# Denominator product a tile sooner on GpSimd, and head sums and normalised queries ahead of the first gated slice on VectorE, in the middle tiles of the forward gated layers

## The chip, the cores and the metric

The kernel runs on one core of one Trainium2 chip. TensorE (PE; its weight loads are shown apart as PEld), VectorE (DVE), ScalarE (ACT) and GpSimd (POOL) each run a program of their own, in order; SyncE (SP) issues the DMAs. The metric is the device time of one execution in microseconds, and for several executions their median.

## The reference

A stack of four layers over x (2048 rows of 512, bfloat16): linear attention (A), gated unit (B), A, B, each on the normalised input and with a residual. Both A share their weights, and so do both B. The outputs are the result and the gradients of x and of the five weight matrices for a given gradient of the result.

```python
def _A_ref(x, wqkv, wo):                  # 32 heads of 16
    q, k, v = split(x @ wqkv)
    phi = lambda t: jnp.where(t > 0, t + 1, jnp.exp(t)) + 1e-6
    pq, pk = phi(q), phi(k)
    kv = jnp.einsum("bhsd,bhse->bhde", pk, v)
    z = jnp.einsum("bhsd->bhd", pk)
    num = jnp.einsum("bhqd,bhde->bhqe", pq, kv)
    den = jnp.einsum("bhqd,bhd->bhq", pq, z)[..., None] + 1e-6
    return heads_joined(num / den) @ wo

def _B_ref(x, w_gate, w_up, w_down):      # 512 -> 1376 -> 512
    g, u = x @ w_gate, x @ w_up
    return (_sigmoid(g) * u) @ w_down

x = x + _A_ref(_layernorm(x), A_wqkv, A_wo)
x = x + _B_ref(_layernorm(x), B_w_gate, B_w_up, B_w_down)
...
```

The part that matters here is `den`: for each row and head, the sum over 16 columns of pq times z, and the division by it.

## The kernel before

The rows are cut into 16 tiles of 128. The layers are numbered 0 (A), 1 (B), 2 (A), 3 (B). `kq_fwd` makes keys, queries and the sums of a whole A layer (`A.zb` holds z in every row, `A.pq_all` the queries). `ab_fwd` then runs over the 16 tiles of the following B layer and does the rest of the A layer a few tiles ahead of it. It runs once for layers 0 and 1 and once for 2 and 3. The backward passes and the weight gradients follow.

Inside `ab_fwd`, engines TensorE, VectorE, ScalarE and GpSimd are under a manual schedule: each runs its instructions in the order in which the code writes them. All DMAs of this part go through SP, in written order too. An instruction that waits holds up everything behind it on its engine.

The pieces, for tile `st` of the B layer:

- `A.prod(st + FLAG)`, with FLAG = 3: one product on GpSimd, pq times z for the tile three ahead, into one of two `prod` buffers (L840).
- `A.front1(st + FLAG)`: the sum over the 16 columns of each head, on VectorE (L846).
- `A.front2(st + FLAG)`: epsilon and reciprocal (L850, L851) and the queries times the reciprocal (`pqnstage`, L863), on VectorE; after every odd tile a DMA stores two tiles of them (L867).
- `A.front3(st + FLAG)`: four TensorE transposes of the normalised queries (L374) and a ScalarE copy (L383).
- `A.attn_y(st + YLAG)`, with YLAG = 2: four matmuls (L884), the residual add on VectorE (L892), and the normalisation sums of that tile: two instructions on VectorE (L449, L451) and three small ones on GpSimd (L452, L453, L455).
- `gu(T, hT, fs)`: one of three slices of the gated unit (512, 512 and 352 columns): gate and up matmuls into a `g` and a `u` bank of PSUM, two buffers each (L922); two sigmoids on ScalarE (L924, L926); up times sigmoid on VectorE, which frees the `u` bank (`hh_t`, L929); a product for the backward pass on GpSimd (`ssd_t`, L930).
- `finish(T)`: the down projection of a tile two before (L956) and its residual add on VectorE (L958). In layer 1 the normalisation sums for layer 2 follow (`nxt.stats`, again L449 to L455); in layer 3 there is no next layer and `nxt` is None.
- `ln.apply`, `ln.stage_T`: the normalised input of a coming tile, on ScalarE, and its transposes.
- `dma_T(T)`: the transpose of `hh_t` by DMA (L949), followed on SP by the stores of `ssd_t` and `hh_t` (L1051, L1052, L1054).

`by_dma` holds the middle tiles, 2 to 14, in both layers. For them the code begins with a memset of a pad of `hh_t` (L982); that tile has three buffers in layer 1 and two in layer 3, so the memset and the first slice may have to wait until the stores of an earlier tile are done. Tiles 0, 1 and 15 have an order of their own. `prod`, `front1` and `front2` do nothing for a tile number of 16 or more, so in middle tiles 13 and 14 they are empty.

Of the kernel before, what the change touches and what calls it, by code (L numbers as in the profile page):

```python
# [35 lines left out]
def fchunks_of_slice(fs):  # L36
    c0, w = FSL[fs]
    return list(range(c0 // P, (c0 + w + P - 1) // P))


def fc_rows(fc):
    return FLAST if fc == NFC - 1 else P


def rows(st):
    return slice(st * P, (st + 1) * P)
# [9 lines left out]
def ps_tile(k, which, shape, dt, name):  # L56
    return k.ps[which].tile(shape, dt, name=name, tag="ln_tp" if which == "ln" else f"{which}_ps")
# [766 lines left out]
FLAG = 3  # L824
# [78 lines left out]
def ab_fwd(k, A, ln, side, nxt=None, out_cb=None, last_cb=None):  # L903
    nc, tc = k.nc, k.tc
    la, l = A.l, A.l + 1
    sva, sv = k.sv[la], k.sv[l]
    with ExitStack() as ctx:
        work = ctx.enter_context(tc.tile_pool(name=f"bf_work{l}", bufs=2, reuse_waits="tile"))
        wide = ctx.enter_context(tc.tile_pool(name=f"bf_wide{l}", bufs=2, reuse_waits="tile"))
        if out_cb is not None:  # L910
            k.ostg = ctx.enter_context(tc.tile_pool(name="out0_stg", bufs=2, reuse_waits="tile"))

        by_dma = HH_DMA[l]

        def gu(T, hT, fs, later=False):
            c0, w = FSL[fs]
            ssd_t, hh_t = T["ssd"], T["hh"]
            g_ps = ps_tile(k, "g", [P, 512], F32, "g_ps")
            u_ps = ps_tile(k, "u", [P, 512], F32, "u_ps")
            for ps, w_sb in ((g_ps, k.wg), (u_ps, k.wu)):  # L920
                for kc in range(NDC):
                    nc.tensor.matmul(ps[:, 0:w], lhsT=hT[:, kc, :], rhs=w_sb[:, kc, c0:c0 + w],  # L922
                                     start=(kc == 0), stop=(kc == NDC - 1))
            nc.scalar.activation(ssd_t[:, 0, c0:c0 + w], g_ps[:, 0:w], ACT.Sigmoid)  # L924
            oms = work.tile([P, 512], BF16, name="oms")
            nc.scalar.activation(oms[:, 0:w], g_ps[:, 0:w], ACT.Sigmoid, scale=-1.0)  # L926

            def rest():
                nc.vector.tensor_tensor(hh_t[:, c0:c0 + w], u_ps[:, 0:w], ssd_t[:, 0, c0:c0 + w], ALU.mult)  # L929
                nc.gpsimd.tensor_tensor(ssd_t[:, 1, c0:c0 + w], hh_t[:, c0:c0 + w], oms[:, 0:w], ALU.mult)  # L930
            if later:
                return rest
            rest()

        def transposes(T, fs):
            hh_t, hhT = T["hh"], T["hhT"]
            fcs = fchunks_of_slice(fs)
            tps = ps_tile(k, "t", [P, 8, P], BF16, "t_tp")
            for i, fc in enumerate(fcs):
                r = fc_rows(fc)  # L940
                nc.tensor.transpose(tps[0:r, i, :], hh_t[:, fc * P:fc * P + r], k.ident[:])
            nfull = len([fc for fc in fcs if fc_rows(fc) == P])
            if nfull > 0:
                nc.scalar.copy(hhT[:, fcs[0]:fcs[0] + nfull, :], tps[:, 0:nfull, :])
            if nfull < len(fcs):
                nc.scalar.copy(hhT[0:FLAST, NFC - 1, :], tps[0:FLAST, nfull, :])

        def dma_T(T):
            nc.sync.dma_start(out=T["hhT"][:], in_=T["hh"][:], transpose=True)  # L949

        def finish(T, bank="y"):
            st = T["st"]
            y_ps = ps_tile(k, bank, [P, D], F32, "y_ps")
            for fc in range(NFC):
                r = fc_rows(fc)
                nc.tensor.matmul(y_ps[:], lhsT=T["hhT"][0:r, fc, :], rhs=k.wd[0:r, fc, :],  # L956
                                 start=(fc == 0), stop=(fc == NFC - 1))
            nc.vector.tensor_tensor(k.xs[st][:], y_ps[:], k.xs[st][:], ALU.add)  # L958
            if nxt is not None:
                nxt.stats(st)  # L960
            ready.append(st)

        ready = []

        def after(upto):
            while ready and ready[0] <= upto:
                st = ready.pop(0)
                if nxt is not None:
                    nxt.apply(st)
                if out_cb is not None:  # L970
                    out_cb(st)

        todo = []
        for st in range(NST):
            hT = ln.pop(st)
            T = dict(st=st,
                     ssd=wide.tile([P, 2, F], BF16, name="ssd_t"),
                     hh=wide.tile([P, FP], BF16, name="hh_t", bufs=3 if l == 1 else 2),
                     hhT=wide.tile([P, NFC, P], BF16, name="hhT"))
            late = st - 1 in by_dma or st in by_dma  # L980
            if st in by_dma:
                nc.gpsimd.memset(T["hh"][:, F:FP], 0.0)  # L982
                A.prod(st + FLAG)
                gu(T, hT, 0)
                A.attn_y(st + YLAG)
                A.front1(st + FLAG)
                A.front2(st + FLAG)
                if todo and todo[0]["st"] <= st - 1 - (st - 1 in by_dma):
                    finish(todo.pop(0), "t")
                after(st - 3)  # L990
                gu(T, hT, 1)
                ln.stage_T(st + 1, "scalar")
                gu(T, hT, 2)
            elif st == 0:
                rest0 = gu(T, hT, 0, True)
                A.front2(2)
                rest0()
                gu(T, hT, 1)
                ln.apply(1)
                A.front3(2, "t")  # L1000
                rest2 = gu(T, hT, 2, True)
                ln.stage_T(1)
                rest2()
                A.front1(FLAG)
                A.attn_y(2)
                transposes(T, 0)
                A.front2(FLAG)
            else:
                A.prod(st + FLAG)
                gu(T, hT, 0)  # L1010
                if st == 1:
                    ln.apply(YLAG)
                else:
                    A.attn_y(st + YLAG)
                if late:
                    finish(todo.pop(0), "t")
                after(st - 2 - late)
                gu(T, hT, 1)
                if st == 1:
                    A.front3(FLAG)  # L1020
                transposes(T, 0)
                if st == 1:
                    A.attn_y(FLAG)
                else:
                    ln.stage_T(st + 1)
                A.front1(st + FLAG)
                gu(T, hT, 2)
                if st == 1:
                    ln.stage_T(2)
                A.front2(st + FLAG)  # L1030
            if l == 1 and st == NST - 1:
                nc.scalar.activation(k.tab[:], k.neg[:], ACT.Exp)
            if st not in by_dma:
                transposes(T, 1)
            if st > 0:
                ln.apply(st + YLAG)
            if st == NST - 1:
                if last_cb is not None:
                    last_cb(0)
                if nxt is not None:  # L1040
                    nxt.early_T()
            if st not in by_dma and todo:
                after(st - 2)
                finish(todo.pop(0))
            if st > 0:
                A.front3(st + FLAG, "t" if st in by_dma else "ln")
            if st in by_dma:
                dma_T(T)
            else:
                transposes(T, 2)  # L1050
            nc.sync.dma_start(out=sv["ssd"][rows(st), :, :], in_=T["ssd"][:])  # L1051
            nc.sync.dma_start(out=sv["hdd"][0:NG, :, st, :].rearrange("g p w -> p g w"),  # L1052
                              in_=T["hh"][:, 0:NG * GW].rearrange("p (g w) -> p g w", g=NG))
            ins = nc.sync.dma_start(out=sv["hdl"][0, :, st, :], in_=T["hh"][:, NG * GW:F])  # L1054
            if st in side:
                with tc.issue_after(ins.ins):
                    side[st]()
            todo.append(T)
        if out_cb is not None:
            out_cb(NST - 2)  # L1060
        if last_cb is not None:
            last_cb(1)
        finish(todo.pop(0))
        if out_cb is not None:
            out_cb(NST - 1)
# [838 lines left out]
```

## Time and profile before

| | us |
|---|---|
| median of 3 runs | 1137.57 |
| the three runs | 1137.09, 1137.57, 1140.26 |
| profiled execution, its own time | 1138.25 |
| its span, first to last instruction | 1136.5 |

| instruction in the profile | count | median ns |
|---|---|---|
| L840 product, GpSimd | 30 | 1153 |
| L846 head sums, VectorE | 32 | 654 |
| L850 epsilon, VectorE | 32 | 181 |
| L851 reciprocal, VectorE | 32 | 353 |
| L863 normalised queries, VectorE | 32 | 692 |

The forward gated layers take the stretches from about 70 to 206 us and from about 262 to 400 us of the span. Times below are microseconds from the start of the span. A row of the timeline gives start, duration, engine, line, operation, the tile written and those read, and in brackets the engine's idle time before it and what ended it. "x2" is two neighbours shown as one row. VectorE's instructions overlap a little, so the distance from start to start is shorter than the duration.

### The profile page before, as it was taken

The page shows a single profiled execution, that of the slowest core. Times are in us where ns is not written, and L with a number is a line of the kernel's source. Part 1 is how long each engine was busy: PE and PEld are TensorE (multiplying, and loading weights), DVE is VectorE, ACT ScalarE, POOL GpSimd, SP SyncE. Part 2 cuts the span into 40 slices and gives each one's busy share as a digit, 9 for nine tenths or more (in the row PEclk, how much of TensorE's full clock was granted, in tenths as well). Part 3 has the DMA queues.
Part 4 walks back from the last instruction along what each step waited for, and adds up shares of the span by engine and source line. Part 5 has one row for each costly group of instructions (what it writes and reads, how often), then busy time and mean ns, then how long its engine had stood idle before and what let it go on. Part 6 is the DMA issues. An engine that isn't in the chain of part 4 may idle for free. (4 is left out here: it accounts for less than half of the span.)

```text
span 1136.5 us, 20007 instructions
## 1 busy us (share of the span) xinstructions
PE 1112.9 (98%) x7468; PEld 650.7 (57%) x7468; DVE 696.3 (61%) x1344; ACT 483.8 (43%) x909; POOL 292.9 (26%) x518
## 2 busy tenths in 40 slices
PE   8989999998999999999999999999999999999998
PEld 4444554444545555554446468855547745448887
DVE  6787876777667466664975850166674976951111
ACT  6666666555755633433625431224324515410000
POOL 5647776435666400000110220000000111210000
PEclk9999999999999999999999999999999999999999
DMA  8967999855899989997899997799998899979996
GB/s 270 310 194 213 288 263 277 250 141 174 228 267 286 269 260 254 303 260 201 224 263 310 220 254 234 210 277 287 248 286 256 209 276 291 239 200 298 266 194 187
DMA packets 413682, 282.36 MB, mean 248 GB/s; under 512 B 198608, under 2 KB 399504, under 8 KB 409744
## 3 DMA queue, kind: packets, MB, share of 16 engines
q1 hardware_dynamic: 413584, 281.08, 89.8%
q8 instruction: 58, 0.95, 0.3%
q14 instruction: 40, 0.33, 0.1%
HBM read 125.44 MB, written 115.70 MB: 212 GB/s over the span
## 5 line engine op out<-in xcount | busy, mean ns | idle before, releaser
L1509 PE MATMUL p_ps<-p_set,p_a 128*128 128x256 bf16 (+1 forms) x2032 | 210.1, 264 | 1.0 <-DMA p_set<-sv_dqk 1.0
L1509 PEld LDWEIGHTS <-p_a 128*128 128x128 bf16 x2048 | 185.9, 98 | 23.4 <-DMA p_set<-sv_dqk 1.2
L1130 DVE TENSOR_TENSOR dd<-dhh_ps,ssd 128x512 bf16<-128x512 f32 x144 | 82.4, 628 | 121.9 <-PE dhh_ps L1108 116.4
L922 PEld LDWEIGHTS <-hT 128*128 128x128 bf16 x768 | 73.2, 98 | 66.4 <-issue 2.9
L1250 PEld LDWEIGHTS <-ddT 128*128 128x128 bf16 (+1 forms) x704 | 67.5, 98 | 74.8 <-DMA ddT<-dd 2.1
L930 POOL TENSOR_TENSOR ssd_t<-hh_t,oms 128x512 bf16<-128x512 bf16 (+1 forms) x96 | 100.1, 1052 | 38.7 <-ACT hT L383 16.9
L1082 POOL TENSOR_SCALAR ab<-c 128x2 f32<-128x2 f32 x64 | 12.4, 194 | 376.4 <-DVE junk L1079 363.1
L1209 ACT COPY ddT<-T_ps 128x1024 bf16<-128x1024 bf16 (+1 forms) x72 | 58.7, 818 | 115.1 <-PE T_ps L1207 62.2
L929 DVE TENSOR_TENSOR hh_t<-u_ps,ssd_t 128x512 bf16<-128x512 f32 (+1 forms) x96 | 59.3, 631 | 60.3 <-PE u_ps L922 36.7
L1074 ACT ACTIVATE t_sb<-dh_ps,rstd_all 128x512 f32<-128x512 f32 x64 | 44.0, 687 | 116.0 <-issue 65.1
L924 ACT ACTIVATE ssd_t<-g_ps 128x512 bf16<-128x512 f32 (+1 forms) x96 | 53.3, 556 | 91.1 <-PE g_ps L922 84.2
L922 PE MATMUL g_ps<-wg,hT 128*128 128x512 bf16 (+1 forms) x384 | 91.5, 361 | 0.0
L922 PE MATMUL u_ps<-wu,hT 128*128 128x512 bf16 (+1 forms) x384 | 90.3, 358 | 0.0
L1483 DVE TENSOR_TENSOR dw_stg<-p_ps,dw_stg 128x512 bf16<-128x512 f32 (+3 forms) x43 | 28.1, 653 | 99.3 <-PE p_ps L1509 82.6
L1250 PE MATMUL dh_ps<-wgT,ddT 128*128 128x512 bf16 (+1 forms) x352 | 85.2, 379 | 0.0
L1250 PE MATMUL dh_ps<-wuT,ddT 128*128 128x512 bf16 (+1 forms) x352 | 81.3, 379 | 0.8 <-DMA ddT<-dd 0.7
L956 PE MATMUL y_ps<-wd,hhT 128*128 128x512 bf16 (+1 forms) x352 | 81.3, 379 | 0.6 <-DVE x L958 0.6
L1493 PE MATMUL p_ps<-p_a,p_set 128*128 128x512 bf16 (+1 forms) x352 | 81.2, 379 | 0.0
L1108 PE MATMUL dhh_ps<-wdT,gTb 128*128 128x512 bf16 x336 | 74.2, 357 | 0.0
L956 PEld LDWEIGHTS <-hhT 128*128 128x128 bf16 (+1 forms) x352 | 34.2, 98 | 41.1 <-issue 0.7
L926 ACT ACTIVATE oms<-g_ps 128x512 bf16<-128x512 f32 (+1 forms) x96 | 52.8, 550 | 2.3 <-POOL ssd_t L930 1.0
L1079 DVE SCALAR_TENSOR_TENSOR junk<-t_sb,h_ld 128x512 bf16<-128x512 f32 x48 | 36.4, 758 | 28.2 <-ACT t_sb L1074 23.3
(227 smaller groups left out, 1820.1 us busy)
## 6 DMA issues: line engine op xcount, KB each, us to landing
p_set<-sv_hdd SPq DMA_DIRECT2D x30, 1024.0 KB, 6.1
sv_ssd<-ssd_t SPq DMA_DIRECT2D x32, 688.0 KB, 4.1
ssd<-sv_ssd SPq DMA_DIRECT2D x24, 688.0 KB, 5.1
sv_hdd<-dd SPq DMA_DIRECT2D x24, 512.0 KB, 4.5
sv_hdd<-hh_t SPq DMA_DIRECT2D x32, 320.0 KB, 4.3
p_a<-sv_h SPq DMA_DIRECT2D x16, 512.0 KB, 6.2
p_set<-sv_dqk SPq DMA_DIRECT2D x8, 1024.0 KB, 7.4
h_ld<-sv_h SPq DMA_DIRECT2D x24, 256.0 KB, 4.7
```

Source lines behind the costliest of these rows:

```text
L922: nc.tensor.matmul(ps[:, 0:w], lhsT=hT[:, kc, :], rhs=w_sb[:, kc, c0:c0 + w], start=(kc == 0), stop=(kc == NDC - 1))
L924: nc.scalar.activation(ssd_t[:, 0, c0:c0 + w], g_ps[:, 0:w], ACT.Sigmoid)
L926: nc.scalar.activation(oms[:, 0:w], g_ps[:, 0:w], ACT.Sigmoid, scale=-1.0)
L929: nc.vector.tensor_tensor(hh_t[:, c0:c0 + w], u_ps[:, 0:w], ssd_t[:, 0, c0:c0 + w], ALU.mult)
L930: nc.gpsimd.tensor_tensor(ssd_t[:, 1, c0:c0 + w], hh_t[:, c0:c0 + w], oms[:, 0:w], ALU.mult)
L956: nc.tensor.matmul(y_ps[:], lhsT=T["hhT"][0:r, fc, :], rhs=k.wd[0:r, fc, :], start=(fc == 0), stop=(fc == NFC - 1))
L1108: k.nc.tensor.matmul(ps[:, 0:w], lhsT=gT[:, jc, :], rhs=k.wdT[:, jc, c0:c0 + w], start=(jc == 0), stop=(jc == NDC - 1))
L1130: k.nc.vector.tensor_tensor(dd_part(dd, a, fs), ps[:, 0:w], ssd[:, a, c0:c0 + w], ALU.mult)
L1209: nc.scalar.copy(out[:, :, 0:nfull, :], tps[:, :, 0:nfull, :])
L1250: nc.tensor.matmul(T["dh"][:], lhsT=T["ddT"][0:r, dd_block(a, fc), :], rhs=(k.wuT, k.wgT)[a][0:r, fc, :], start=(i == 0), stop=(i == 2 * N ...
L1493: nc.tensor.matmul(ps[0:r, :], lhsT=set_t[:, st, c * P:c * P + r], rhs=self.ops[j["l"], "g"][:, st, :], start=(st == 0), stop=(st == NST - 1))
L1509: nc.tensor.matmul(ps[:, icl * w:(icl + 1) * w], lhsT=self.ops[j["l"], "h"][:, st, ic * P:(ic + 1) * P], rhs=set_t[:, st, 0:w], start=(st ...
```

## The change

In the middle tiles `front1` and `front2` stand in front of the first slice and the residual add instead of behind them. Their product is issued at the end of the tile before (tile 1 included, which issues two: its own and that of tile 2), after `ln.apply` and in front of what follows there.

```diff
             if st in by_dma:
                 nc.gpsimd.memset(T["hh"][:, F:FP], 0.0)
-                A.prod(st + FLAG)
+                A.front1(st + FLAG)
+                A.front2(st + FLAG)
                 gu(T, hT, 0)
                 A.attn_y(st + YLAG)
-                A.front1(st + FLAG)
-                A.front2(st + FLAG)
                 if todo and todo[0]["st"] <= st - 1 - (st - 1 in by_dma):
                     finish(todo.pop(0), "t")
                 after(st - 3)
...
             if st > 0:
                 ln.apply(st + YLAG)
+            if st + 1 in by_dma:
+                A.prod(st + 1 + FLAG)
             if st == NST - 1:
```

## The prediction

> **What bounds the kernel now.** I read the busy shares first, then busy time tile by tile, then the instructions of GpSimd and VectorE in order of time through one tile of each gated layer, and last the waits of TensorE for normalised queries.
>
> ```profile
> PE 1112.9 (98%) x7468; PEld 650.7 (57%) x7468; DVE 696.3 (61%) x1344; ACT 483.8 (43%) x909; POOL 292.9 (26%) x518
> ```
>
> TensorE is busy for 98% of the span. The middle tiles of the forward gated layers are what the change touches; these three rows are one tile of layer 1 and two of layer 3 (stretch, length, busy time of PE, PEld, DVE, ACT, POOL, clock, DMA share, GB/s):
>
> ```profile
> 119.23:127.57 8.34, 8.34 (x51) 4.25 (x49) 6.57 (x14) 5.46 (x11) 6.38 (x12) 1.00 1.11 333
> 327.53:336.00 8.47, 8.27 (x46) 3.94 (x43) 4.04 (x9) 5.38 (x11) 4.87 (x8) 1.00 1.06 337
> 345.19:353.53 8.34, 8.34 (x51) 4.26 (x49) 5.87 (x11) 5.16 (x11) 5.40 (x9) 1.00 1.11 286
> ```
>
> TensorE fills 8.34 us of 8.34: it sets the pace, so an engine's share says nothing against another order as long as no loop through the other engines exceeds 8.34 us. In layer 1 GpSimd has 6.4 us of work in it and VectorE 6.6, so such a loop is near. The tile on GpSimd, then on VectorE:
>
> ```profile
> 122.04 1.16 POOL L840 TENSOR_TENSOR prod<-pq_all,zb 128x512 bf16<-128x512 bf16 x1
> 127.19 0.23 POOL L452 TENSOR_SCALAR rstd_all<-ln_mv 128x1 f32<-128x1 f32 x1 [1.50 <-DVE ln_mv L451]
> 128.39 1.96 POOL L930 TENSOR_TENSOR ssd_t<-hh_t,oms 128x512 bf16<-128x512 bf16 x2
> 130.29 0.13 POOL L982 MEMSET hh_t<- 128x32 bf16 x1
> 130.38 1.16 POOL L840 TENSOR_TENSOR prod<-pq_all,zb 128x512 bf16<-128x512 bf16 x1
> ```
>
> ```profile
> 122.02 0.69 DVE L892 TENSOR_TENSOR x<-y_ps,x_bf 128x512 f32<-128x512 f32 x1
> 123.58 0.65 DVE L846 TENSOR_REDUCE den<-prod 128x32 f32<-128x512 bf16 x1
> 125.48 0.68 DVE L958 TENSOR_TENSOR x<-y_ps,x 128x512 f32<-128x512 f32 x1
> 126.92 0.18 DVE L451 BATCH_NORM_AGGREGATE ln_mv<-ln_stats 128x2 f32<-128x6 f32 x1
> 127.02 1.12 DVE L929 TENSOR_TENSOR hh_t<-u_ps,ssd_t 128x512 bf16<-128x512 f32 x2
> 129.55 0.69 DVE L929 TENSOR_TENSOR hh_t<-u_ps,ssd_t 128x512 bf16<-128x512 f32 x1 [1.41 <-PE u_ps L922]
> ```
>
> GpSimd runs behind. Its product starts at 130.38, straight after the last slice of the tile before (the memset costs 0.09), and ends at 131.53, though VectorE has finished its last slice at 128.14 and begins the new first slice at 129.55. Today that does no harm: the head sums (L846) come after the first slice and the residual add, 0.38 us after the product's end in the tile shown (123.20 to 123.58).
>
> Where the normalised queries are late now, TensorE says:
>
> ```profile
> 102.33 0.40 PE L374 MATMUL t_ps<-ident,pqnstage 128*128 128x128 bf16 x4 [0.65 <-DVE pqnstage L863]
> 293.82 0.40 PE L374 MATMUL t_ps<-ident,pqnstage 128*128 128x128 bf16 x4 [0.48 <-DVE pqnstage L863]
> 336.53 0.40 PE L374 MATMUL t_ps<-ident,pqnstage 128*128 128x128 bf16 x4 [0.73 <-DVE pqnstage L863]
> ```
>
> 1.86 us in all: tile 3 of either layer, which has no down projection to fill it, and tile 8 of layer 3.
>
> **The change, part by part.** Nothing is added or removed. Eleven products, eleven head sums, reciprocals and normalisations per layer (for tiles 2 to 12) move.
>
> *GpSimd.* The product goes from behind the memset to in front of it. Both stand behind the same last slice, so it comes 0.09 us sooner, not a tile, except where the memset waits for a store of layer 3 (2.27 and 3.24 us at 306.22 and 332.33). At tile 1 it passes the normalisation sums of the down projection: they wait until 88.62, and the product, at 89.89 now, can start at 86.4. GpSimd issues no DMA here. On SP the store of normalised queries (L867, every second tile) still stands between the tile before and this tile's DMA transpose, and passes no DMA: 0, hidden by TensorE's tile.
>
> *VectorE.* The four instructions from L846 to L863 take 1.90 us (123.58 to 125.48). Moved ahead of the first slice they would fit the 1.41 us idle there, nearly, if the product were done. It is not. So VectorE waits for it with the first slice, the residual add, both normalisation sums and the other slices queued behind; GpSimd waits for those slices and sums, TensorE for the up-projection bank (two buffers) that the second slice frees. That closes a loop from product to product. Layer 1, from rows of this trace: hand-off 0.03 (GpSimd to VectorE at 1004.43); head sums to normalised queries 1.90; first slice 0.61 (98.13 to 98.74); residual add and sums 1.56 (122.02 to 123.58); down-projection add and sums 1.62 (125.48 to 127.10); hand-off 0.09; three small GpSimd instructions 1.20 (127.19 to 128.39); two slices 1.90 (128.39 to 130.29); product 1.15. Sum 10.06 us against TensorE's 8.33: 1.73 a tile. The same from the other side: first slice, add and sums, 2.17, are inserted in a loop with 0.4 us of slack, 1.77. I take 1.75.
>
> The unknown of this sum is how the same instructions space out when late. Lowest, product by its spacing (1.11, 130.38 to 131.49) and no hand-off: 10.0, 1.65 a tile; highest, a product of 1.53 (at 278.12) and 0.80 for a first slice (129.55 to 130.36): 10.6, 2.3. The middle rows repeat in every tile, so 1.75 stands.
>
> The Trainium skill, page "Perfetto Trace Analysis", section "GPSIMD Engine Instruction", holds a GpSimd instruction's reported span unreliable and would have spacings taken. The row gives 1.15 by span and 1.11 by spacing; by the rule alone the whole sum would be some 0.7 us smaller.
>
> *Layer 1 tile by tile.* Product 5 ends at 87.6, so the head sums follow the down projection's sums at 88.45; the first slice of tile 2 goes from 89.44 to 90.35. The next product ends at 98.6, first slice of tile 3 at 100.55 (now 98.13), second at 102.7, done 103.4. There TensorE no longer waits 0.65 for the queries but for the up-projection bank, and is where it is now (103.42). Product 107.15, first slice of tile 4 at 109.1 (now 104.55), second slice at 112.9, done 113.6; TensorE wants that bank at 111.76: 1.85 late. Then 8 tiles more (5 to 12) at 1.75: 14.0. Tile 13 has no queries and TensorE is dense again. Layer 1: +15.85.
>
> *Layer 3.* No sums follow the down projection here (no next layer), so GpSimd waits for the second slice instead: 0.03 + 1.90 + 0.61 + 1.56 + 0.66 (the add) + 0.82 (second slice to GpSimd's start, 337.00 to 337.82) + 1.90 + 1.15 = 8.63, 0.3 a tile over TensorE. The 0.48 at tile 3 again turns into the bank's wait. At tiles 5 and 8 the first slice waits for a store today anyway (306.34, 332.32), which hides part of the lag: reckoned on, TensorE is 0.85 late after tile 4, 1.0, 1.3, 1.6, then 0.9 after tile 8 (whose own 0.73 stall is gone), and 2.2 after tile 12. Ends: 0.5, if adds take 0.60 and product 1.11; 4.5, if the stores move with the slices and each of the waits at tiles 5, 8 and 11 grows by 0.8.
>
> Sum: 15.85 + 2.2 = +18.0 us. What follows is TensorE-bound (571.57 busy in 576.5 us from 560 on), so it reaches the end. The profiled execution took 1138.25 us (span 1136.5, 1.75 around it), 0.68 over the median 1137.57 and inside the three runs: 1138.25 + 18.0 = 1156.3, or 1155.6 from the median. I say 1156. Ends: 13.2 (8 x 1.65) + 1.5 (tile 4, less 0.35) + 0.5 = +15, 1153; 18.4 (8 x 2.3) + 2.2 + 4.5 = +25, 1163.
>
> **The rivals.** *Not slower.* The product ends before VectorE is through with the last slice; then the head sums fill the 1.41 us idle and the three stalls go: 1138.25 - 1.9 = 1136.4. It decides at 128.14 in the tile shown: the product would have to end 3.4 us sooner than 131.53. Only GpSimd's order could do that, and the product stands behind slices which it runs until 130.29. That the move does nothing is excluded for the same reason: VectorE's order changes. 0.06.
>
> *The clock falls.* TensorE would idle 1.75 us in each 10 us tile of layer 1. After gaps of 1.63 and 1.23 us close together the granted clock was 0.87 in 60 to 70, and four matmuls took 1.91 us (68.49) instead of 1.03; with one gap of 1.72 us in 40 to 50 it stayed 1.00. If half of each tile ran so, TensorE's 8.33 becomes 12.5, 2.4 over the loop, 8 tiles: +19 more, 1175. The single gap per tile is nearest to the second row: 0.05. The Trainium skill, "TensorE: Matmul & The Clock Gate", section "A second HAM failure mode: psum-queue depth-cycling", describes short idles between matmul groups that make the clock alternate; by that rule this rival would come about, and the 40 to 50 row speaks against it.
>
> *Layer 3's stores bind.* Its gated tiles have two buffers; if late slices make every first slice from tile 5 on (8 of them) wait 0.6 us more for a store: +5, 1161. The stores that bind today are held by weight loads, not by slices: 0.07.
>
> **How the numbers follow.** Forecast 0.82 (1153 to 1163), not slower 0.06, clock 0.05, stores 0.07. The range 1150 to 1164 holds the forecast and the stores, with 1 to 3 us for the spread of runs (1137.09 to 1140.26); it leaves out the clock and the not-slower case. 0.3% (3.4 us) is about what a measurement here tells from no change: faster 0.01 (the stalls total 0.17%), within 0.05, slower 0.94.
>
> **What would show it.** In the changed profile VectorE's idle before the head sums (L846) has GpSimd's product as releaser, some 1.5 to 2 us in each tile of layer 1; TensorE stands before the first slice's up matmuls, released by VectorE; product to product is 10.1 us in layer 1 and 8.6 in layer 3; the stalls before the query transposes are gone. It is wrong if layer 1's period stays 8.33, or if the head sums start before 128.5 in the tile shown.

## The result, and the profile after

| | before | after |
|---|---|---|
| median, us | 1138.91 (1137.09 to 1140.36, 4 runs) | 1155.86 (1155.19 to 1157.2, 4 runs) |
| profiled execution, us | 1138.25 | 1156.21 |
| its span, us | 1136.5 | 1154.5 |

The ratio is 1.0151, 95% interval 1.0138 to 1.0164. Between the two profiled executions lie 17.96 us, between the medians 16.95 (the kernel before has a fourth run by now, of 1140.36).

The busy shares of the changed kernel, from its page (busy us, share of the span, instructions of each engine):

```profile
PE 1109.9 (96%) x7358; PEld 649.7 (56%) x7468; DVE 693.9 (60%) x1344; ACT 486.2 (42%) x909; POOL 290.3 (25%) x518
```

No engine has more instructions than before: the busy times differ by a few us at most, and TensorE's 3 us less goes with 110 matmul records that are missing. The span is longer because TensorE stands. One tile of layer 1 and one of layer 3 after, busy time by stretch (stretch, length, busy time of PE, PEld, DVE, ACT, POOL, clock, DMA share, GB/s):

```profile
129.66:139.74 10.08, 8.44 (x48) 4.24 (x47) 6.46 (x14) 5.68 (x11) 6.38 (x12) 1.00 0.85 254
342.60:351.20 8.60, 8.47 (x48) 4.19 (x48) 5.60 (x12) 5.38 (x11) 5.40 (x8) 1.00 1.11 303
```

A tile of layer 1 takes 10.08 us where it took 8.34, with 6.46 us of work on VectorE (6.57 before) and the same 6.38 on GpSimd; the clock stays at 1.00. GpSimd and VectorE in that tile, in order of time (start, duration, engine, line, operation, tile written and tiles read, and in brackets the idle time before it and what ended it):

```profile
125.58 1.15 POOL L840 TENSOR_TENSOR prod<-pq_all,zb 128x512 bf16<-128x512 bf16 x1
...
132.54 0.23 POOL L452 TENSOR_SCALAR rstd_all<-ln_mv 128x1 f32<-128x1 f32 x1 [0.27 <-DVE ln_mv L451]
...
133.75 1.96 POOL L930 TENSOR_TENSOR ssd_t<-hh_t,oms 128x512 bf16<-128x512 bf16 x2
135.66 1.15 POOL L840 TENSOR_TENSOR prod<-pq_all,zb 128x512 bf16<-128x512 bf16 x1
```

```profile
126.77 0.69 DVE L846 TENSOR_REDUCE den<-prod 128x32 f32<-128x512 bf16 x1 [3.38 <-POOL prod L840]
128.70 0.68 DVE L929 TENSOR_TENSOR hh_t<-u_ps,ssd_t 128x512 bf16<-128x512 f32 x1
...
130.85 0.66 DVE L958 TENSOR_TENSOR x<-y_ps,x 128x512 f32<-128x512 f32 x1
131.54 0.70 DVE L449 BATCH_NORM_STATS2 ln_stats<-x 128x6 f32<-128x512 f32 x1
132.27 0.18 DVE L451 BATCH_NORM_AGGREGATE ln_mv<-ln_stats 128x2 f32<-128x6 f32 x1
132.37 1.10 DVE L929 TENSOR_TENSOR hh_t<-u_ps,ssd_t 128x512 bf16<-128x512 f32 x2
136.85 0.69 DVE L846 TENSOR_REDUCE den<-prod 128x32 f32<-128x512 bf16 x1 [3.38 <-POOL prod L840]
```

These rows show a loop with no slack in it. The product ends at 126.73 and the head sums start at 126.77. From there VectorE runs without a gap to the second and third slice (132.37 to 133.47). GpSimd takes the normalisation sums at 132.54, its two slice products follow, and straight behind them the next product. VectorE's one idle time in the tile is the 3.38 us in which it waits for that product. TensorE's idle times in these tiles are rows of one kind:

```profile
112.93 1.02 PE L922 MATMUL u_ps<-wu,hT 128*128 128x512 bf16 x4 [0.37 <-DVE hh_t L929]
123.01 1.02 PE L922 MATMUL u_ps<-wu,hT 128*128 128x512 bf16 x4 [1.58 <-DVE hh_t L929]
133.09 1.02 PE L922 MATMUL u_ps<-wu,hT 128*128 128x512 bf16 x4 [1.59 <-DVE hh_t L929]
143.17 1.02 PE L922 MATMUL u_ps<-wu,hT 128*128 128x512 bf16 x4 [1.58 <-DVE hh_t L929]
```

It stands in front of the up matmuls until VectorE frees the bank. In the list of TensorE's waits (what waited, for what, us in total, times, longest) these have become the largest entry; the list before has no such entry:

```profile
PE u_ps L922 <- DVE hh_t L929: 14.1, 12, 1.8
PE y_ps L884 <- ACT pqnT L383: 3.5, 4, 1.1
```

Layer 3's tile takes 8.60 us. There TensorE stands elsewhere. The list of waits of its weight loads in 300 to 395 us has an entry that the list before has not:

```profile
PEld L884 <- ACT pqnT L383: 6.7, 10, 1.5
```

The attention matmuls (L884) wait for the copy of the transposed queries (L383). That copy stands on ScalarE behind the normalisation, which itself waits for GpSimd's last small instruction, itself behind VectorE's late sums:

```profile
345.43 0.81 ACT L460 ACTIVATE hstage<-x,ln_nmr,rstd_all 128x512 bf16<-128x512 f32 x1 [0.43 <-POOL ln_nmr L455]
346.15 0.56 ACT L383 COPY pqnT<-t_ps 128x512 bf16<-128x512 bf16 x1
```

Where the 18 us arise can be read from the start of the down projection (L956), the same instruction in both traces. What the changed kernel is behind, in us, at the layer's first one, at that of each tile from 4 on (tile 3 has none), and at the layer's last:

| | first | tile 4 | 5 | 6 | 7 | 8 | 9 | 10 | 11 | 12 | 13 | last |
|---|---|---|---|---|---|---|---|---|---|---|---|---|
| layer 1 | -0.61 | 0.64 | 1.17 | 2.91 | 4.66 | 6.41 | 8.15 | 9.91 | 11.65 | 13.41 | 15.15 | 15.15 |
| layer 3 | 15.41 | 16.66 | 16.89 | 17.02 | 17.27 | 17.52 | 16.78 | 17.04 | 17.29 | 17.56 | 17.81 | 17.80 |

Layer 1 costs 15.76 us (15.15 + 0.61), layer 3 2.39 us, and 0.26 us lies between. At the end of the span it is 18.0.

### The profile page after: what moved, and what is told of

Its sections match the earlier page's. It is cut to its first block, busy times and chain, and to the rows that moved or that the text cites. A ratio compares the mean times of both kernels' runs of the same rounds, so it can differ in the third digit from the quotient of the medians.

```text
span 1154.5 us, 19901 instructions
## 1 busy us (share of the span) xinstructions
PE 1109.9 (96%) x7358; PEld 649.7 (56%) x7468; DVE 693.9 (60%) x1344; ACT 486.2 (42%) x909; POOL 290.3 (25%) x518
## 5 line engine op out<-in xcount | busy, mean ns | idle before, releaser
L956 PE MATMUL y_ps<-wd,hhT 128*128 128x512 bf16 (+1 forms) x340 | 80.6, 379 | 1.2 <-DVE x L958 0.6
L1109 PE MATMUL dhh_ps<-wdT,gTb 128*128 128x512 bf16 (+1 forms) x323 | 72.5, 356 | 0.6
L846 DVE TENSOR_REDUCE den<-prod 128x32 f32<-128x512 bf16 x32 | 21.8, 681 | 61.4 <-POOL prod L840 61.3
L956 PEld LDWEIGHTS <-hhT 128*128 128x128 bf16 (+1 forms) x352 | 34.2, 98 | 41.1 <-issue 0.7
```

The lines of the kernel that those rows point to most:

```text
L1109: k.nc.tensor.matmul(ps[:, 0:w], lhsT=gT[:, jc, :], rhs=k.wdT[:, jc, c0:c0 + w], start=(jc == 0), stop=(jc == NDC - 1))
```

## The experiments

The theory: the change closes a loop through VectorE and GpSimd, from product to product; its length sets the pace wherever it is over TensorE's 8.33 us. The rivals: the 1.9 us of sums and normalised queries in front of the first slice are late for TensorE by themselves, wherever the product is; or TensorE's clock falls from standing. The first four kernels ran beside the kernel before at 1138.57 us, the last four at 1138.63. All diffs are against the changed kernel.

**The product a place sooner.** Sums and queries stay in front of the first slice. Each tile issues the next tile's product right behind its own `attn_y`, so on GpSimd the product stands behind the normalisation sums of that `attn_y` and ahead of the second and third slice's products.

```diff
                 A.attn_y(st + YLAG)
+                if st + 1 in by_dma:
+                    A.prod(st + 1 + FLAG)
...
-            if st + 1 in by_dma:
+            if st == 1:
                 A.prod(st + 1 + FLAG)
```

> The order of the changed kernel, but GpSimd issues the product behind the normalisation sums that follow the residual add of the tile before, ahead of the down projection's sums and of the second and third slice; there it has 1.50 us of idle time in layer 1 for the 1.11 us of a product. Theory (the loop from product to product, closed because the product stands behind the slices): the loop opens, TensorE runs at 8.33 us a tile in both layers, and the stalls before the query transposes (1.86 us) go: 1136 to 1138 us, 0 to 2 us under the kernel before. Rival (the 1.90 us of head sums and normalised queries ahead of the first slice cost by themselves, since VectorE had only 1.41 us idle there): at least 0.5 us a tile stays, 11 tiles in two layers, 1147 to 1156 us. Rival (gaps lower TensorE's clock): no gaps, no statement.

Measured: 1135.45 us, ratio 0.9976 (0.9965 to 0.9988). A tile of layer 1 and one of layer 3, busy time by stretch:

```profile
125.28:133.67 8.39, 8.33 (x48) 4.29 (x48) 7.35 (x14) 5.55 (x11) 6.36 (x12) 1.00 1.07 337
328.61:336.94 8.33, 8.28 (x47) 4.26 (x47) 5.59 (x12) 6.35 (x13) 5.19 (x8) 1.00 0.96 293
```

TensorE is dense again with the sums in the same early place. So the block of 1.9 us in front of the first slice does not cost by itself; the wait for the product does. By the starts of the down projection it gains 0.60 us in layer 1 and 1.79 in layer 3 against the kernel before, mostly where that kernel's query transposes stalled, in tile 3 of each layer and in tile 8 of layer 3 (0.60 between the down projections of tiles 2 and 4; in layer 3 0.66 there, 0.13 between those of tiles 5 and 6 and 1.00 between those of 8 and 9). It is the fastest kernel here, by less than the 0.3% that was called measurable ahead, though with 12 runs its interval stays below 1.

**The product between the second and third slice's.** The loop is shortened by one place only.

```diff
                 gu(T, hT, 1)
+                if st + 1 in by_dma:
+                    A.prod(st + 1 + FLAG)
                 ln.stage_T(st + 1, "scalar")
...
-            if st + 1 in by_dma:
+            if st == 1:
```

> The order of the changed kernel, but the product stands between GpSimd's products of the second and the third slice. Loop theory: the loop is shorter by the third slice's 0.80 us; layer 1 at 10.08 - 0.80 = 9.28 us a tile, 0.95 over TensorE, 8 tiles and some 1.0 before them: +8.6; layer 3 at 8.59 - 0.80 = 7.79, under TensorE, so it costs nothing and loses its stalls, -1.2: together +7.4, 1145 to 1148 us. Rival (the block ahead of the first slice costs by itself): as the changed kernel, 1156 us.

Measured: 1145.5 us, ratio 1.0058 (1.0043 to 1.0074). The head sums on VectorE in three tiles of layer 1:

```profile
125.07 0.69 DVE L846 TENSOR_REDUCE den<-prod 128x32 f32<-128x512 bf16 x1 [2.57 <-POOL prod L840]
134.34 0.69 DVE L846 TENSOR_REDUCE den<-prod 128x32 f32<-128x512 bf16 x1 [2.57 <-POOL prod L840]
143.61 0.69 DVE L846 TENSOR_REDUCE den<-prod 128x32 f32<-128x512 bf16 x1 [2.57 <-POOL prod L840]
```

The period is 9.27 us, 0.81 less than 10.08, and layer 3's is 8.33: its loop has fallen under TensorE's pace. VectorE still waits 2.57 us for GpSimd in each tile of layer 1. The loop's length is what counts, not the wait's.

**Each half of the change alone.** First the product's move, with sums and queries back behind the first slice and the residual add:

```diff
-                A.front1(st + FLAG)
-                A.front2(st + FLAG)
                 gu(T, hT, 0)
                 A.attn_y(st + YLAG)
+                A.front1(st + FLAG)
+                A.front2(st + FLAG)
```

> Only the product moves, to the end of the tile before; head sums and normalised queries stay behind the first slice and the residual add. Loop theory: the product starts 0.09 us sooner (the memset) and nobody waits for it any more or less: within 1 us of the kernel before, 1137 to 1140 us. Rival (the product's new place on GpSimd costs, since it passes the down projection's sums at tile 1 and the memset): slower by more than 0.3%.

Measured: 1138.77 us, ratio 0.9997 (0.9987 to 1.0007): nothing. Then the sums' move, with the product back behind the memset:

```diff
                 nc.gpsimd.memset(T["hh"][:, F:FP], 0.0)
+                A.prod(st + FLAG)
                 A.front1(st + FLAG)
...
-            if st + 1 in by_dma:
-                A.prod(st + 1 + FLAG)
```

> Only the head sums and normalised queries move ahead of the first slice; the product stays behind the memset at the head of the tile. Loop theory: layer 1 at 10.08 + 0.09 us a tile, and its first product ends at 91.0 instead of 88.0 us (behind the down projection's sums), so the loop starts some 3 us later: +19.5; in layer 3 0.09 a tile more, and the memset's wait for stores (2.3 and 3.2 us in the kernel before) now stands in the loop: +3 to +6. Together 1161 to 1165 us, 5 to 9 over the changed kernel. Rival (the block ahead of the first slice costs by itself, whenever the product comes): as the changed kernel, 1156 us.

Measured: 1161.23 us, ratio 1.02 (1.0187 to 1.0213). The whole loss comes from the sums' move; given that, the product's move saves 5 us. GpSimd's memset and product show part of where:

```profile
128.09 0.13 POOL L982 MEMSET hh_t<- 128x32 bf16 x1
128.17 1.16 POOL L840 TENSOR_TENSOR prod<-pq_all,zb 128x512 bf16<-128x512 bf16 x1
...
138.33 1.16 POOL L840 TENSOR_TENSOR prod<-pq_all,zb 128x512 bf16<-128x512 bf16 x1
```

```profile
341.80 1.15 POOL L840 TENSOR_TENSOR prod<-pq_all,zb 128x512 bf16<-128x512 bf16 x1
352.05 0.12 POOL L982 MEMSET hh_t<- 128x32 bf16 x1 [1.62 <-DMA sv_hdl<-hh_t]
352.13 1.15 POOL L840 TENSOR_TENSOR prod<-pq_all,zb 128x512 bf16<-128x512 bf16 x1
```

With the memset in the loop layer 1's period is 10.15 to 10.16 us in place of 10.08, and in layer 3 one tile of 10.33 arises where the memset waits for a store. By the starts of the down projection, layer 1 loses 18.94 us instead of 15.76, and 2.7 of the difference lies between the down projections of tiles 2 and 4: the product that the changed kernel starts at the end of tile 1, at 85.79, starts here in tile 2 at 89.10, and its head sums follow at 90.28 instead of 87.84. Layer 3 loses 4.86 instead of 2.39.

In this kernel alone TensorE's clock did drop within the middle tiles, in 104 to 108 us (the mean of 100 to 110 is 0.83), just behind idle times of 0.60 us (ending at 96.61) and 2.06 us. Four up matmuls that take 1.02 us elsewhere took 1.91:

```profile
103.10 0.76 PE L922 MATMUL u_ps<-wu,hT 128*128 128x352 bf16 x4 [2.06 <-DVE hh_t L929]
103.92 1.70 PE L922 MATMUL g_ps<-wg,hT 128*128 128x512 bf16 x4
105.41 1.91 PE L922 MATMUL u_ps<-wu,hT 128*128 128x512 bf16 x4
```

The loop does not show it: the products on either side (99.24 and 107.88) are 8.63 us apart, and so are those of layer 3's same tiles (307.08 and 315.71), where the clock is 1.00. So the drop lengthened no turn of the loop, and the loss stays the loop's.

**The product twice.** This lengthens the loop by one known instruction.

```diff
             if st + 1 in by_dma:
                 A.prod(st + 1 + FLAG)
+                A.prod(st + 1 + FLAG)
```

> The changed kernel with the product at the end of the tile issued twice (the second copy is the one that is read; nothing is left out). Loop theory: the loop from product to product is lengthened by the product's spacing, 1.11 us: layer 1 from 10.08 to 11.19 a tile, layer 3 from 8.59 to 9.70. Eight to nine tiles each: 9 x 1.11 in layer 1, and in layer 3 nine tiles of 1.37 over TensorE's 8.33 in place of 0.26, so some 10 + 10 more: 1175 to 1180 us. Rival, GpSimd has room for it (6.5 us busy in a tile of 10.08, so 3.6 free): no change, 1156. Rival, longer standing times make the granted clock fall: TensorE then stands 2.9 us in each tile of layer 1, and if the clock falls for it the matmuls last longer than 1.03 for four and the time is over 1185.

Measured: 1179.02 us (1177.32 to 1184.22), ratio 1.0367 (1.0344 to 1.039). The products, two in a row, and then two tiles by stretch:

```profile
130.12 2.26 POOL L840 TENSOR_TENSOR prod<-pq_all,zb 128x512 bf16<-128x512 bf16 x2
141.32 2.26 POOL L840 TENSOR_TENSOR prod<-pq_all,zb 128x512 bf16<-128x512 bf16 x2
152.51 2.26 POOL L840 TENSOR_TENSOR prod<-pq_all,zb 128x512 bf16<-128x512 bf16 x2
```

```profile
141.32:152.51 11.19, 8.66 (x48) 4.24 (x47) 6.46 (x13) 5.68 (x11) 7.49 (x14) 1.00 0.76 210
152.51:163.70 11.19, 8.65 (x48) 4.25 (x47) 6.46 (x13) 5.67 (x11) 7.49 (x14) 1.00 0.52 150
```

1.11 us more work on an engine that is idle for 3.7 us of each tile makes each tile 1.11 us longer, in layer 1 (11.19 against 10.08) and in layer 3 (9.70 against 8.59). The clock rival does not explain it: TensorE now stands 1.81 and 0.7 us in each tile, and the granted clock is 1.00.

**The product on VectorE, in the changed kernel's place.**

```diff
             if st + 1 in by_dma:
-                A.prod(st + 1 + FLAG)
+                A.prod(st + 1 + FLAG, nc.vector)
```

> The changed kernel's order, but the product of the middle tiles runs on VectorE in the same place. Loop theory: VectorE no longer waits for GpSimd's last slices, so the loop is open; VectorE's work in a tile of layer 1 grows from 6.6 to about 7.0 us, under 8.33. Periods 8.33 to 8.4, stalls of the query transposes in tile 3 gone: 1134 to 1138 us. Rival, the sums and normalised queries ahead of the first slice cost by themselves (now 2.3 us with the product): first slice late in every tile, 1145 or more.

Measured: 1137.29 us, ratio 0.9989 (0.9978 to 1.0001). VectorE now has the product in front of the sums, 2.3 us or more ahead of the first slice, and the down projections still follow each other at 8.33 to 8.34 us. With the product off GpSimd (which is thereby relieved of 1.15 us a tile), the wait for GpSimd's last slices is out of VectorE's way, and the loss is gone. VectorE itself is not quite at TensorE's pace: its head sums come 8.45 us apart in layer 1 (112.43, 120.87), for a reason shown in the last section, a lag of 0.11 a tile that does not reach TensorE before the layer ends. The stall of the query transposes in layer 1's tile 3 is gone as expected, but in its place TensorE waits 0.59 us in front of the attention matmuls at 104.57, so that layer gains next to nothing.

**The change in layer 3 alone.**

```diff
             if st in by_dma:
                 nc.gpsimd.memset(T["hh"][:, F:FP], 0.0)
-                A.front1(st + FLAG)
-                A.front2(st + FLAG)
+                if l == 3:
+                    A.front1(st + FLAG)
+                    A.front2(st + FLAG)
+                else:
+                    A.prod(st + FLAG)
                 gu(T, hT, 0)
                 A.attn_y(st + YLAG)
+                if l == 1:
+                    A.front1(st + FLAG)
+                    A.front2(st + FLAG)
...
-            if st + 1 in by_dma:
+            if l == 3 and st + 1 in by_dma:
```

> The changed order in layer 3 alone; layer 1 as in the kernel before. Loop theory: layer 1 without delay, layer 3 with its period of 8.59 and +2.1 us at its end, the same as inside the full change: 1140 to 1141.5 us, ratio 1.0018. Rival, layer 3's +2.1 comes of arriving late from layer 1 (the stores of normalised queries or of the gated tiles stand otherwise then): period 8.33 and no loss, 1137 to 1138.5.

Measured: 1139.87 us, 0.1 under the expected range, ratio 1.0019 (1.001 to 1.0029). A tile of layer 1 and one of layer 3:

```profile
129.72:138.06 8.34, 8.34 (x49) 4.27 (x48) 6.57 (x14) 5.46 (x11) 6.38 (x12) 1.00 1.02 256
331.25:339.85 8.60, 8.52 (x49) 4.19 (x48) 5.59 (x11) 5.95 (x12) 5.41 (x9) 1.00 0.86 265
```

Layer 3 has its 8.60 without a late layer 1 ahead of it. By the starts of the down projection it loses 2.41 us, against 2.39 inside the full change: its loss is the same with and without a late layer 1 ahead of it. This kernel is also 0.68 us early at 84 us, ahead of anything that differs from the kernel before, so the changed kernel's 0.61 there is no gain of its order either.

**The early product with sums in the old place.**

```diff
-                A.front1(st + FLAG)
-                A.front2(st + FLAG)
                 gu(T, hT, 0)
                 A.attn_y(st + YLAG)
+                if st + 1 in by_dma:
+                    A.prod(st + 1 + FLAG)
+                A.front1(st + FLAG)
+                A.front2(st + FLAG)
...
-            if st + 1 in by_dma:
+            if st == 1:
```

> The early product (issued for the next tile between the first and second slice's product on GpSimd, as in the run that did so with the sums ahead), but head sums and normalised queries behind the first slice and the residual add, as in the kernel before. It shows where the 0.24% of that run comes from. If from the sums standing ahead (queries ready sooner for TensorE's transposes in tiles 3 and 8): like before, 1137.5 to 1139. If from the product alone: 1135 to 1136.

Measured: 1139.5 us, ratio 1.0009 (0.9999 to 1.0018), 0.5 us over what was expected of no gain. So the gain of the first experiment needs both halves: product early, and with it sums early.

## Why the prediction was right

- *TensorE sets the pace at 8.33 us, so only a longer loop can cost.* Right. Where the loop is open or shorter, the down projections follow each other at 8.33 to 8.34 us; where it is longer, at the loop's length. Two loops that are only just longer, 8.39 and 8.45 us (last section), did not reach TensorE within a layer.
- *The product is not a tile sooner; the move is worth 0.09 us a tile.* Right: 0.07 to 0.08 where the sums are early, nothing where they are not. The larger part of what the move saves lies at tile 1 (2.7 us), which the tile-by-tile reckoning had in its start of 86.4; it came at 85.79, which is 86.40 less the 0.61 us that this execution is early there, and took 1.60 us instead of 1.15.
- *The loop of layer 1, 10.06 us.* 10.08 was measured. By the rows above and their neighbours: product and hand-off 1.19 (1.18 put down), sums to normalised queries 1.93 (1.90), first slice 0.60 (0.61), residual add and sums 1.55 (1.56), down-projection add and sums with its hand-off 1.69 (1.71), small GpSimd instructions 1.21 (1.20), two slices 1.91 (1.90).
- *1.75 a tile, +15.85 in layer 1.* The table gives 13.98 for the eight tiles between the down projections of 5 and 13, 1.75 each, and 1.78 ahead of them (1.85 put down). The split of these 1.78 was wrong. Behind tile 3 TensorE was to be "where it is now", its 0.65 us stall turned into the wait for the up bank, and 1.85 late behind tile 4. It was 1.25 late by tile 4's down projection and lost 0.53 more by tile 5's: by the first of these it had waited, besides the up bank (0.24 us at 100.72 and 0.29 at 102.84), 1.05 us in front of the attention matmuls at 104.92 for the copy of the transposed queries, which that step had left out.
- *Layer 3, loop 8.63 us, +2.2.* 8.59 and +2.39 were measured. The course is as reckoned but for its start: 1.48 late by tile 5's down projection where 0.85 was put down after tile 4, then 0.13 to 0.27 a tile instead of 0.3, and 0.74 back at tile 8, whose own stall goes. The place was wrong: from tile 4 on TensorE waits there mainly for the transposed queries (1.05 us at 312.43, where the up bank cost 0.29 at 310.36), and from tile 5 on for them alone. The loop sets the sum, whichever of its late results TensorE meets first.
- *Stores.* The rival that layer 3's stores bind fell: its products follow each other at 8.56 to 8.60, and only one memset waited (0.39 us at 348.84). In the kernel with the sums' move alone one such wait did reach the pace.
- *The clock.* Fell for the changed kernel: 1.00 with a gap of 1.59 us in each tile, and with two gaps in each tile of the doubled product. That it can drop here the sums' move alone showed, once, behind idle times of 0.60 and 2.06 us; why it did not behind the doubled product's 1.93 us at 103.02 stays open. The rule of the Trainium skill that was cited for it ("TensorE: Matmul & The Clock Gate", "A second HAM failure mode: psum-queue depth-cycling") names short idles between matmul groups that make the clock alternate; the regular gaps of these two kernels don't.
- *What was to be seen.* VectorE's idle before the head sums was put at 1.5 to 2 us and is 3.38 in layer 1. The 1.75 that a tile grows by was taken for the whole wait. Idle time that VectorE had elsewhere in the tile, 1.41 us before the first slice, is gathered in it as well: 1.41 + 1.75 is 3.16, most of the 3.38. The other signs came as said: the product as releaser, TensorE standing before the first slice's up matmuls until VectorE frees the bank, periods of 10.08 and 8.59, and no stall before the query transposes of tile 3 and of layer 3's tile 8.
- *The span of a GpSimd instruction.* The sums start 0.04 us after the product's reported end (126.73 to 126.77), so the reported end is what a waiting engine sees here. The rule of the Trainium skill on such spans ("Perfetto Trace Analysis", "GPSIMD Engine Instruction") would have taken 0.7 us off the sum; the span gave the loop to 0.02 us.
- *The sum.* +18.0 was put down, 17.96 came between the profiled executions and 16.95 between the medians. That the first agrees to 0.04 us is luck. Layer 1 cost 0.1 less and layer 3 0.2 more than reckoned; the 0.61 early at the start, the 0.26 between the layers and 0.2 behind them belong to no part of the sum and happen to cancel nearly.

## What to carry to other kernels

Before an instruction is moved ahead on an in-order engine, follow the ring: what it waits for, what that stands behind on its own engine, and whether one of those waits for something now queued behind the moved instruction. Add up the ring from rows of the trace and compare it with the pace of the bottleneck; busy shares say nothing of it, as 1.11 us added to an engine with 3.7 us idle showed. A consumer gains from standing earlier only if its producer is taken out of the ring first; here one place further up on GpSimd turned 1.5% of loss into 0.2% of gain.

## What the runs showed of the hardware that was not expected

Some instructions of VectorE and GpSimd hold each other up whole. With the product on VectorE, its duration in layer 1 grows from tile to tile, although it starts every 8.34 us. VectorE's product and, at the same time, GpSimd's slice products:

```profile
111.68 0.71 DVE L840 TENSOR_TENSOR prod<-pq_all,zb 128x512 bf16<-128x512 bf16 x1
120.02 0.82 DVE L840 TENSOR_TENSOR prod<-pq_all,zb 128x512 bf16<-128x512 bf16 x1
...
161.69 1.38 DVE L840 TENSOR_TENSOR prod<-pq_all,zb 128x512 bf16<-128x512 bf16 x1
170.03 0.41 DVE L840 TENSOR_TENSOR prod<-pq_all,zb 128x512 bf16<-128x512 bf16 x1
```

```profile
110.95 2.14 POOL L930 TENSOR_TENSOR ssd_t<-hh_t,oms 128x512 bf16<-128x512 bf16 x2
119.40 2.15 POOL L930 TENSOR_TENSOR ssd_t<-hh_t,oms 128x512 bf16<-128x512 bf16 x2
...
161.63 2.14 POOL L930 TENSOR_TENSOR ssd_t<-hh_t,oms 128x512 bf16<-128x512 bf16 x2
170.08 2.19 POOL L930 TENSOR_TENSOR ssd_t<-hh_t,oms 128x512 bf16<-128x512 bf16 x2
```

Whenever VectorE's product starts behind GpSimd's pair, it ends 1.44 us after the pair's start: 112.39 less 110.95, 120.84 less 119.40, 163.07 less 161.63. That is 1.03 us, about the first of the two GpSimd products, and then its own 0.41. So a loop is left in this kernel too: the head sums follow the product, GpSimd's small instructions and its pair follow VectorE's sums, and the next product waits for the first of the pair. It takes 8.45 us (110.95 to 119.40), 0.11 over TensorE's pace, and the wait grows by that in each tile. At 170.03 the product starts 0.05 us ahead of the pair and takes 0.41; then the pair takes 2.19, where the pair of the kernel before takes 1.96. The Trainium skill, page "SBUF — State Buffer", section "🔬 SBUF: two separate sides", says that the two engines share a pair of ports under an exclusive lock, held for the whole instruction by whichever starts first; these rows agree with it.

It also meets a small instruction. In the kernel with the early product, epsilon and normalised queries fall beside GpSimd's slices:

```profile
128.15 0.76 DVE L850 TENSOR_SCALAR den<-den 128x32 f32<-128x32 f32 x1
129.33 0.90 DVE L863 TENSOR_TENSOR pqnstage<-pq_all,rden_all 128x512 bf16<-128x512 bf16 x1
```

0.76 and 0.90 us, against the medians of 0.18 and 0.69 before. So in layer 1 of that kernel it is 2.71 us from the head sums to the start of the first slice (127.44 to 130.15) instead of 1.93, GpSimd's product and VectorE's normalised queries come at 8.39 us a tile against TensorE's 8.33, and VectorE's busy time in a tile is 7.35 us instead of 6.46. TensorE was not reached by that lag in the tiles that a layer has; what it would cost over more of them was not measured.
